# Routing tables made tile by tile, weight loads that wait for a gather, and two copies on another engine

## The chip, the cores and the metric

The kernel runs on one core of a Trainium2 chip. The metric is the device time of one launch in microseconds; it is the median of several runs.

## The reference

Attention, then a routed expert layer, then a dense layer. The shapes are 4 batches x 12 heads x 448 rows x 64; 1792 tokens of 768 numbers; 8 experts with room for 224 tokens each, 768 to 1024 to 768; and a dense 768 to 2048 to 768.

```python
q_n, k_n = rmsnorm(q, g_q), rmsnorm(k, g_k)
attn = softmax(q_n @ k_n.T / 8)
x = tokens(attn @ v)                       # 1792 x 768

cap = N // E                               # 224
logits = x @ w_gate                        # 1792 x 8
for idx in np.argsort(-logits.flatten()):  # best pairs first
    tok, e = idx // E, idx % E
    if assigned[tok] >= 0 or counts[e] >= cap:
        continue
    assigned[tok] = e
    counts[e] += 1
for e in range(E):
    out[assigned == e] = np.maximum(x[assigned == e] @ w1[e], 0) @ w2[e]

h = out @ w_in
return np.where(h > 0, h, np.exp(np.minimum(h, 0)) - 1) @ w_out
```

Every token ends with exactly one expert, and each expert with exactly 224 tokens. The loop over all pairs is sequential; the kernel finds the same assignment in another way.

## The kernel before, in words

The program has four stages: attention (to about 280 us), the routing (280 to 309), the eight experts, and the dense layer. Weights and operands are kept as a high and a low f16 part, and each product is made of three f16 matmuls.

**Routing.** The token's logits lie as L, 128 partitions x 14 token tiles x 8 experts. A round (`round_`, called five times) lets each token choose its best expert (`choose`, oh), and then raises the prices of the experts that are too full (`raises`). For that it counts, for each expert, how many of its tokens would stay at each of 128 price steps. The count is a sum of matmuls, one for each token tile: the weights are a table of 128 x 128 comparisons (token against step), and the moving operand is oh of that tile, with 8 columns. Two tiles' tables, ga, are made by ScalarE (ACT) with a sign function; twelve tiles' tables, gd, by VectorE (DVE). The counts (cnt) give ind on DVE, and two small matmuls k and q end the round. Between these, TensorE runs filler matmuls named warm on operands that nobody reads. Beside them DVE makes halves of the first expert's low weight parts, named wa (`W.low`), and ACT their high parts (`W.high`).

**Placing.** `place` numbers the tokens of each expert (pre), and splits the number into hi and lo. The tables Pm, 128 tokens x 112 places for each of 14 tiles, are comparisons of lo with the numbers 0 to 111; 14 matmuls (ip) with them give, for each expert and place, the token that belongs there. DVE turns these into idx. It also makes fi, which tells whether the assignment is complete. If it isn't, a conditional block with more rounds runs; on these inputs it is passed by.

**Gather and first expert.** `gather()` fetches the 224 rows of an expert by two indirect DMAs on POOL's queue, into xg, half 1 first and then half 0. It is called for the first expert straight behind the placing, for the second behind the conditional. `columns(0)` then makes f16 parts xh on ACT and DVE, transposes them on TensorE (xt) and copies them to xe; the first expert's matmuls are ph (first layer) and py (second).

**Weights of the later experts.** `W.split` issues a load into a staging tile (fw, five of them), and orders ACT's and DVE's conversions behind `W.after`. The instructions of each engine are ordered by a scheduler, except in the blocks marked `manual_schedule`; `issue_after(x)` makes the scheduler place what is issued in it behind x.

**Queues.** A load by SyncE (SP) goes to one of its eight DMA semaphores DMAHW0 to DMAHW7, indirect DMAs on POOL to DMASW0 and following.

Of the kernel before, what the change touches and what calls it, by code (L numbers as in the profile page):

```python
# [6 lines left out]
F16 = mybir.dt.float16  # L7
I32 = mybir.dt.int32
AF = mybir.ActivationFunctionType
ALU = mybir.AluOpType  # L10
# [10 lines left out]
P = 128  # L21
# [9 lines left out]
def attention(tc, qk_d, v_d, qT_d, g_d, idh, idn_d, R_d, xs, L, route, W, npairs=NP_):  # L31
    nc = tc.nc
    order = [(s.split(":")[0], int(s.split(":")[1])) for s in ORDER.split()]
    with tc.tile_pool(name="ac", bufs=1) as cp, \
# [381 lines left out]
        with tc.manual_schedule():  # L416
            first()
            for t in range(lo_, npairs + hi_):
                if t == 1:
                    gate()  # L420
                turn(t)
                if t == npairs - 5:
                    route.rows()
                if npairs - 4 <= t <= npairs:
                    W.load()

# [70 lines left out]
def host_route():  # L497
    G, D, Q = route_grids()
    p = np.arange(P)
    tok = np.zeros((P, NT + 1), np.float32)  # L500
    tok[:, NT] = np.where(p < P - 1, CAP - 0.5, -1)
    for t in range(NT):
        if t < 12:
            tok[:, t] = (t // 3) * S + (t % 3) * P + p
        else:
            tok[:, t] = (2 * (t - 12) + (p >= 64)) * S + 384 + p % 64
    ar = np.ascontiguousarray
    c16 = np.concatenate([np.broadcast_to(G.reshape(1, -1), (P, 3 * P)), np.triu(np.ones((P, P)), 1), np.ones((P, P)),
                          np.repeat(np.stack([D, Q], 1).reshape(6, P).T, P, axis=1)], axis=1).astype(np.float16)
    rows = np.repeat(np.concatenate([G[0], G[1], np.arange(112, dtype=np.float16)]), 8)  # L510
    return dict(c16=ar(c16), c32=ar(tok), c8=ar(np.broadcast_to(rows, (P, len(rows)))))


class Route:
    def __init__(self, tc, cp, ring, c16_d, c32_d, c8_d):
        self.tc, self.nc = tc, tc.nc
        nc = tc.nc
        self.ring, self.c8_d = ring, c8_d
# [12 lines left out]
    def constants(self):  # L531
        for a, b in self.loads:
            self.nc.sync.dma_start(a, b)

    def rows(self):

        GG = self.ring.tile([P, 2, P, 8], F16, tag="w2", name="GG", bufs=6)
        self.io = self.ring.tile([P, 112, 8], F16, tag="w2", name="io", bufs=6)
        self.GG = [GG[:, n] for n in range(2)]
        self.nc.sync.dma_start(GG.rearrange("p n c t -> p (n c t)"), self.c8_d[:, 0:16 * P])  # L540
        self.nc.sync.dma_start(self.io.rearrange("p c t -> p (c t)"), self.c8_d[:, 16 * P:])

    def windows(self, sp, pp, L):

# [24 lines left out]
    def run(self, L, idx, row_d, W, gather):  # L569
# [9 lines left out]
        with tc.tile_pool(name="rt", bufs=1, reuse_waits="tile") as sp, \  # L579
# [6 lines left out]
            oh, half, ga, gd = T("oh", tile3, F16), T("half", [P, A, 8], F16), T("ga", [P, A, P], F16), T("gd", [P, P, NT - A], F16)  # L586
            U, V, M, s, v, u = T("U", tile3), T("V", tile3), T("M", tile3), T("s", tile3), T("v", [P, NT]), T("u", [P, NT], F16)
# [19 lines left out]
            def raises(X, n, *beside):  # L607


                for h in H:  # L610
                    nc.vector.scalar_tensor_tensor(s[:, h], X[:, h], 1000.0, oh[:, h], ALU.min, ALU.mult)

                nc.scalar.activation(half, oh[:, 0:A], AF.Copy, scale=0.5)
                for h in H:
                    nc.vector.tensor_reduce(u[:, h], s[:, h], AX.X, ALU.max)
                for t in range(A):
                    nc.scalar.activation(ga[:, t], self.G[n], AF.Sign, bias=u[:, t:t + 1], scale=-1.0)
                for h in H:
                    a, b = max(h.start, A), h.stop
                    G = self.GG[n][:, :, 0:b - a] if n < 2 else self.G[n].unsqueeze(2).broadcast_to([P, P, b - a])  # L620
                    nc.vector.tensor_tensor(gd[:, :, a - A:b - A], u[:, a:b].unsqueeze(1).broadcast_to([P, P, b - a]), G, ALU.is_ge)
                for f in beside:
                    f()
                cnt = pp.tile([P, 8], F32, name="cnt", tag="cnt")
                for t in range(A):
                    nc.tensor.matmul(cnt, self.ones, half[:, t], start=t == 0, stop=False)
                for t in range(NT):
                    nc.tensor.matmul(cnt, ga[:, t] if t < A else gd[:, :, t - A], half[:, t] if t < A else oh[:, t], start=False, stop=t == NT - 1)
# [16 lines left out]
            def place(first=lambda: None, second=lambda: None):  # L645
# [13 lines left out]
                r1, pos, hi, lo = T("r1", tile3), T("pos", [P, NT]), T("hi", [P, NT]), T("lo", [P, NT], F16)  # L659
                Pm, Q = T("Pm", [P, 112, NT], F16), T("Qm", [P, NT, 2, 8], F16)  # L660
# [7 lines left out]
                nc.vector.scalar_tensor_tensor(lo, hi, -112.0, pos, ALU.mult, ALU.add)  # L668
                nc.gpsimd.tensor_tensor(Q[:, :, 1], Q[:, :, 0], hi.unsqueeze(2).broadcast_to(tile3), ALU.mult)
                ip = pp.tile([112, 2, 8], F32, name="ip", tag="ip")  # L670
                for h in H:
                    n = h.stop - h.start
                    nc.vector.tensor_tensor(Pm[:, :, h], lo[:, h].unsqueeze(1).broadcast_to([P, 112, n]), self.io[:, :, 0:n], ALU.is_equal)
                nc.vector.tensor_scalar(j, pre[0:1, NT, :], CAP, None, ALU.is_equal)
                nc.vector.tensor_reduce(f, j, AX.X, ALU.add)
                nc.vector.tensor_copy(fi, f)
                second()

                for t in range(NT):
                    nc.tensor.matmul(ip, Pm[:, :, t], Q[:, t], start=t == 0, stop=t == NT - 1)  # L680
# [14 lines left out]
            with tc.manual_schedule():  # L695
                for h in H:
                    nc.vector.tensor_tensor(U[:, h], L[:, h], bc(self.t0, h.stop - h.start), ALU.subtract)
                warm(8)
                round_(0, L, self.iw, W.high, relative)
                for k in range(1, KSTEP):  # L700
                    round_(1, Ln, self.r, W.high, W.low)
                choose(Ln)
                fi = place(lambda: W.low(2), lambda: W.low(4))
                gather()
                W.second(2)
                for k in range(3):
                    W.high()
                    W.low(2)
                warm(3)
# [59 lines left out]
class Weights:  # L769
# [51 lines left out]

    def split(self, tag, bufs, src, n, name):
        nc = self.nc
        f = self.stage(src, n, name)
        w = self.ring.tile([P, 2, n], F16, tag=tag, name=name, bufs=bufs)
        with self.tc.issue_after(self.after):
            nc.scalar.activation(w[:, 0], f, AF.Copy, scale=SW)  # L827
        with self.tc.issue_after(self.after):
            nc.vector.scalar_tensor_tensor(w[:, 1], f, SW, w[:, 0], ALU.mult, ALU.subtract)  # L829
        return w  # L830
# [44 lines left out]
class Rows:  # L875
# [5 lines left out]
    def gather(self, e=0, x=None):  # L881
        x = x or self.first
        for h in (1, 0):
            self.nc.gpsimd.indirect_dma_start(x[h][0:112], None, self.xs, bass.IndirectOffsetOnAxis(ap=self.idx[0:112, h, e:e + 1], axis=0))
        return x


def moe(tc, xp, pre, xs, idx, idh, W, rows, ring, w1_d, w2_d, wi_d, wo_d, lin, g_d, t_d, out):
    nc = tc.nc
    with tc.tile_pool(name="mp", bufs=1, space=PSUM, reuse_waits="tile") as pp:  # L890
# [19 lines left out]
        with tc.tile_pool(name="m1", bufs=1, reuse_waits="tile") as sp:  # L910
# [5 lines left out]
            def columns(e):  # L916
# [9 lines left out]
                for d in range(0, 6, 2):  # L926
                    pt = bank(2 if e == 0 and d == 4 else 0, f"xt{e}_{d}").bitcast(F16)[:, 0:4 * CAP].rearrange("p (d j c) -> p d j c", d=2, j=2)
                    for k in range(2):
                        for h in (1, 0):
                            for j in range(2):  # L930
                                nc.tensor.transpose(pt[:, k, j, 112 * h:112 * h + 112], hl[h][0:112, j, (d + k) * P:(d + k + 1) * P], idh[0:112, 0:112])  # L931
                    last = nc.vector.tensor_copy(x[:, d:d + 2], pt)  # L932
                return last.ins

            def result(e, d, ps):
# [255 lines left out]
```

## Time and profile before

| | |
|---|---|
| runs | 968.62, 969.22, 968.42 us; median 968.62 |
| profiled execution | 968.6 us, span 966.8 us |
| TensorE (PE) busy | 938.5 us, 97% of the span |
| VectorE (DVE) busy | 727.0 us, 75% |
| ScalarE (ACT) busy | 521.8 us, 54% |
| GpSimd (POOL) busy | 295.3 us, 31% |

All times of the trace count from the start of the span. The slices of the page divide the span into 40 equal parts, and a digit 9 means busy for nine tenths or more. In a timeline, each row is one instruction or several like ones in succession (x4), with its start, the time that it covers, and in brackets how long the engine was idle before it and what ended that.

### The profile page before, as it was taken

The page shows a single profiled execution, that of the slowest core. Times are in us where ns is not written, and L with a number is a line of the kernel's source. Part 1 is how long each engine was busy: PE and PEld are TensorE (multiplying, and loading weights), DVE is VectorE, ACT ScalarE, POOL GpSimd, SP SyncE. Part 2 cuts the span into 40 slices and gives each one's busy share as a digit, 9 for nine tenths or more (in the row PEclk, how much of TensorE's full clock was granted, in tenths as well). Part 3 has the DMA queues.
Part 4 walks back from the last instruction along what each step waited for, and adds up shares of the span by engine and source line. Part 5 has one row for each costly group of instructions (what it writes and reads, how often), then busy time and mean ns, then how long its engine had stood idle before and what let it go on. Part 6 is the DMA issues. An engine that isn't in the chain of part 4 may idle for free.

```text
span 966.8 us, 18734 instructions
## 1 busy us (share of the span) xinstructions
PE 938.5 (97%) x6920; PEld 624.0 (65%) x6920; DVE 727.0 (75%) x1424; ACT 521.8 (54%) x1148; POOL 295.3 (31%) x483
## 2 busy tenths in 40 slices
PE   5999999999998999999999999999999999999997
PEld 2465555555554889999999955555555566666664
DVE  6899999899867898787878799999834675555430
ACT  4899998999853666666655243343312323333320
POOL 6889999999521532221000000000000000000000
PEclk8999999999998999999999999999999999999999
DMA  9444434453235788777765377787764563333000
GB/s 333 182 126 124 154 118 139 131 172 91 59 112 162 180 286 280 243 228 244 223 211 178 104 253 254 256 259 263 208 215 124 161 224 112 105 114 99 33 33 33
DMA packets 100640, 164.93 MB, mean 171 GB/s; under 512 B 32960, under 2 KB 66240, under 8 KB 100160
## 3 DMA queue, kind: packets, MB, share of 16 engines
q1 hardware_dynamic: 96336, 152.66, 50.1%
q0 software_dynamic: 2400, 11.01, 3.3%
q8 instruction: 56, 0.92, 0.4%
q10 hardware_dynamic: 1808, 0.01, 0.1%
q14 instruction: 40, 0.33, 0.1%
HBM read 131.66 MB, written 31.99 MB: 169 GB/s over the span
## 4 chain that ended last, share of the span: by engine, by line
PE 88%; DVE 5%; ACT 2%; DMA 2%; issue 1%; POOL 1%; POOLq 0%; DVEq 0%; ACTq 0%
PE l L1076 23%; PE o_b L1123 11%; PE py L997 10%; PE ph L960 10%; PE o L305 8%; PE o_c L1123 6%; PE s L228 6%; PE pt L281 5%; PE o_a L1123 3%; PE s L221 1%; PE pt L279 1%; PE pk L198 1%; DVE w L829 1%; PE xt L931 1%; PE xo L329 1%
## 5 line engine op out<-in xcount | busy, mean ns | idle before, releaser
L1076 PE MATMUL l<-xc,wic 128*128 128x384 f16 (+1 forms) x1152 | 218.2, 353 | 0.0
L1076 PEld LDWEIGHTS <-wic 128*128 128x128 f16 x1152 | 112.7, 98 | 104.8
L1139 POOL DMA_INDIRECT out<-xc,id x14 | 13.7, 982 | 463.7 <-issue 311.7
L1123 PEld LDWEIGHTS <-a 128*128 128x128 f16 x1080 | 105.7, 98 | 69.8
L829 DVE SCALAR_TENSOR_TENSOR w<-fw,w 128x768 f16<-128x768 f32 (+1 forms) x98 | 112.8, 1153 | 25.2 <-ACT w L827 25.1
L997 PE MATMUL py<-h,w 128*128 128x224 f16 x1152 | 113.8, 259 | 1.5 <-DVE h L962 1.5
L233 DVE TENSOR_REDUCE s<-s 128x1 f32<-128x448 f32 x168 | 105.2, 626 | 9.6 <-PE s L228 8.9
L997 PEld LDWEIGHTS <-w 128*128 128x128 f16 x1152 | 109.9, 98 | 1.9 <-issue 1.6
L252 ACT ACTIVATE p<-s,nb,r 128x448 f32<-128x448 f32 x144 | 104.4, 726 | 4.8 <-DVE nb L239 3.5
L960 PE MATMUL ph<-xe,w 128*128 128x224 f16 x1008 | 99.1, 259 | 0.7 <-DVE xe L932 0.4
L960 PEld LDWEIGHTS <-w 128*128 128x128 f16 x1008 | 96.5, 98 | 1.1 <-issue 1.1
L827 ACT ACTIVATE w<-fw 128x768 f16<-128x768 f32 (+1 forms) x98 | 90.7, 928 | 3.2 <-DMA fw<-w 3.0
L290 ACT ACTIVATE e<-pt 128x448 f32<-128x448 f32 (+2 forms) x216 | 83.7, 428 | 15.8 <-PE pt L281 15.2
L1078 ACT ACTIVATE e<-l 128x512 f32<-128x512 f32 (+1 forms) x64 | 34.5, 539 | 100.5 <-PE l L1076 100.5
L305 PE MATMUL o<-e,v 128*64 128x448 f32 x384 | 87.8, 558 | 0.0
L281 PE MATMUL pt<-idn,p 128*128 128x128 f32 x432 | 70.9, 276 | 2.1 <-ACT p L252 1.6
L281 PEld LDWEIGHTS pt<-idn,p 128*128 128x128 f32 x432 | 50.1, 140 | 24.5 <-ACT e L290 16.7
L924 POOL TENSOR_TENSOR xh<-xg,xh 112x768 f16<-112x768 f32 x14 | 25.7, 1853 | 122.3 <-ACT xh L923 122.3
L1053 DVE SCALAR_TENSOR_TENSOR a<-s,a 128x1024 f16<-128x1024 f32 (+2 forms) x30 | 33.4, 1116 | 38.6 <-ACT a L1052 38.6
L228 PE MATMUL s<-ks,qh 128*128 128x448 f16 x144 | 51.8, 360 | 7.6 <-ACT p L252 6.5
L1123 PE MATMUL o_b<-wb,a 128*128 128x384 f16 x312 | 51.8, 326 | 0.0
L228 PE MATMUL s<-ks,ql 128*128 128x448 f16 x144 | 51.4, 357 | 0.0
(244 smaller groups left out, 1605.0 us busy)
## 6 DMA issues: line engine op xcount, KB each, us to landing
fw<-w SPq DMA_DIRECT2D x56, 384.0 KB, 3.8
fw<-w SPq DMA_DIRECT2D x42, 512.0 KB, 4.6
xwi<-wi SPq DMA_DIRECT2D x16, 768.0 KB, 4.7
xwo<-wo SPq DMA_DIRECT2D x16, 768.0 KB, 4.7
q<-g_d SPq DMA_DIRECT2D x24, 512.0 KB, 3.7
qT<-qT SPq DMA_DIRECT2D x24, 448.0 KB, 4.2
qk<-qk SPq DMA_DIRECT2D x23, 448.0 KB, 3.5
g_d<-e SPq DMA_DIRECT2D x32, 256.0 KB, 4.8
```

Source lines behind the costliest of these rows:

```text
L228: nc.tensor.matmul(ps[:, 0:448], q[:, o:o + P], ks[:, 448 * h:448 * h + 448], start=n == 0, stop=n == 1)
L233: nc.vector.tensor_reduce(d["s", u][:, 448:449], d["s", u][:, 0:448], AX.X, ALU.max, negate=True)
L252: nc.scalar.activation(dst, d["s", u][:, 0:448], AF.Exp, bias=d["nb", u], scale=d["r"][:, rc:rc + 1], accum_out=d["sm"][:, rc:rc + 1])
L281: nc.tensor.transpose(pt[:, j * P:(j + 1) * P], p[j][:, h, 64 * h + c * P:64 * h + (c + 1) * P], idn)
L290: move = nc.vector.tensor_copy if u not in (0, 1, 2, 4, 5, 6) else lambda o, x: nc.scalar.activation(o, x, AF.Copy)
L305: nc.tensor.matmul(d["o"][64 * h:64 * h + 64, 0:448], d["v"][:, c + 4 * h, :], d["e", min(2 * c + h, 6)], start=c == 0, stop=c == 3)
L827: nc.scalar.activation(w[:, 0], f, AF.Copy, scale=SW)
L829: nc.vector.scalar_tensor_tensor(w[:, 1], f, SW, w[:, 0], ALU.mult, ALU.subtract)
L960: mm = nc.tensor.matmul(ps, w[:, i, d * P:(d + 1) * P], x[:, d, j], start=d == 0 and n == 0, stop=d == 5 and n == 2)
L997: nc.tensor.matmul(ps, w[:, i, f * P:(f + 1) * P], h[:, f, j], start=f == 0 and n == 0, stop=f == 7 and n == 2)
L1076: nc.tensor.matmul(ps, w[:, i, d * P:(d + 1) * P], xc[cb][:, h, d, j], start=d == 0 and m == 0, stop=d == 5 and m == 2)
L1123: nc.tensor.matmul(ps, a[x][:, f, i], wt[b][f][:, j], start=first and f == 0 and k == 0, stop=f == 7 and k == 2, skip_group_check=True)
```

## The change

- **Tables of a round.** gd and Pm are laid out by token tile, so that one tile's table is contiguous. Each tile's table is made by one DVE operation that compares a whole row of steps with one number per partition: u for gd (12 operations instead of 2 in a round), lo for Pm (14 instead of 2). u and lo become f32. The 14 count matmuls stand in another order.
- **Constants.** The repeated tables GG and io, loaded in attention's last part, are gone. A small io of 112 numbers is loaded instead.
- **Loads of the second expert.** gather() of the first expert is followed by a DMA of one number from the gathered half 0 to a scratch row. It is named `W.behind`, and all loads in `W.split` are ordered behind it.
- **Copies.** For the first expert, two of three copies of xe (d = 0 and 4) go to ACT.

```diff
-                for h in H:
-                    a, b = max(h.start, A), h.stop
-                    G = self.GG[n][:, :, 0:b - a] if n < 2 else ...
-                    nc.vector.tensor_tensor(gd[:, :, a - A:b - A], u[:, a:b].unsqueeze(1).broadcast_to([P, P, b - a]), G, ALU.is_ge)
+                for t in range(A, NT):
+                    nc.vector.tensor_scalar(gd[:, t - A], self.G[n], u[:, t:t + 1], None, ALU.is_le)
...
-                for t in range(NT):
-                    nc.tensor.matmul(cnt, ga[:, t] if t < A else gd[:, :, t - A], ...)
+                for t in (2, 3, 4, 5, 0, 6, 7, 8, 9, 1, 10, 11, 12, 13):
+                    nc.tensor.matmul(cnt, ga[:, t] if t < A else gd[:, t - A], ...)
...
-                for h in H:
-                    n = h.stop - h.start
-                    nc.vector.tensor_tensor(Pm[:, :, h], lo[:, h].unsqueeze(1).broadcast_to([P, 112, n]), self.io[:, :, 0:n], ALU.is_equal)
+                for t in range(NT):
+                    nc.vector.tensor_scalar(Pm[:, t], io, lo[:, t:t + 1], None, ALU.is_equal)
...
-                gather()
+                W.behind = nc.sync.dma_start(row_d[0:1, 0:1], gather()[0][0:1, 0:1]).ins
...
     def split(self, tag, bufs, src, n, name):
         nc = self.nc
-        f = self.stage(src, n, name)
+        with self.tc.issue_after(self.behind):
+            f = self.stage(src, n, name)
...
-                    last = nc.vector.tensor_copy(x[:, d:d + 2], pt)
+                    last = nc.scalar.activation(x[:, d:d + 2], pt, AF.Copy) if e == 0 and d != 2 else nc.vector.tensor_copy(x[:, d:d + 2], pt)
```

The instructions as they stand in the built programs show three places. The first is DVE in one of the later rounds, from the maxima u to ind. Before:

```order
L615 TENSOR_REDUCE u<-s 128x6
L615 TENSOR_REDUCE u<-s 128x8
L621 TENSOR_TENSOR gd<-u,GG 128x128x4
L621 TENSOR_TENSOR gd<-u,GG 128x128x8
L794 SCALAR_TENSOR_TENSOR wa_4913<-fa_4160,wa_4913 128x384
L629 TENSOR_SCALAR ind<-cnt,c_72 128x8
```

And DVE in the same round of the changed kernel:

```order
L606 TENSOR_REDUCE u<-s 128x6
L606 TENSOR_REDUCE u<-s 128x8
L610 TENSOR_SCALAR gd<-c_71,u 128x128 x12
L782 SCALAR_TENSOR_TENSOR wa_4921<-fa_4156,wa_4921 128x384
L618 TENSOR_SCALAR ind<-cnt,c_72 128x8
```

Twelve operations stand where two stood; the half of wa behind them, and ind behind that, have not moved.

The second place is SP at the conditional, with what each instruction waits for (fi is the flag of the placing; fw_1_0 and fw_1_1 are the first two weight loads of the second expert). Before:

```order
L694 TENSOR_LOAD fi [waits DVE_49]
L694 ISA x2
L819 DMA fw_1_0_6975<-w 128x768 [waits DMAHW2_49,DVE_49,Activation_49]
L819 DMA fw_1_1_7001<-w 128x768 [waits DMAHW3_49,DVE_49,Activation_49]
L711 COMPARE_AND_BRANCH
...
L711 UNCONDITIONAL_BRANCH [waits SP_sequencer_49,DMAHW0_49,DMAHW1_49,DMAHW2_49,DMAHW3_49,DMAHW4_49,DMAHW5_49,DMAHW6_49,DMAHW7_49]
```

And SP in the changed kernel:

```order
L682 TENSOR_LOAD fi [waits DVE_49]
L682 ISA x2
L692 DMA row<-xg_0_4826 1x1 [waits DMAHW1_49,DMASW1_49]
L807 DMA fw_1_0_7100<-w 128x768 [waits DMAHW2_49,DVE_49,Activation_49]
L807 DMA fw_1_1_7126<-w 128x768 [waits DMAHW3_49,DVE_49,Activation_49]
L699 COMPARE_AND_BRANCH
```

The copy to row stands ahead of both loads and waits for DMASW1, the semaphore of the gather's second DMA. The loads still stand ahead of the conditional, behind which SP waits for all eight of its semaphores.

The third place is ACT behind the conditional, with its waits: the f16 parts xh of the gathered halves. Before:

```order
L923 ACTIVATE xh_1_6541<-xg_1_4831 112x256 [waits DMASW2_49,DMAHW5_49,DMASW0_49,DVE_49]
L923 ACTIVATE xh_1_6541<-xg_1_4831 112x256 x2
L923 ACTIVATE xh_0_6540<-xg_0_4830 112x256 [waits DMASW3_49,DMASW1_49,DVE_49]
L923 ACTIVATE xh_0_6540<-xg_0_4830 112x256 x2
L953 DMA lin<-ix_6509 112x16x1 [waits DMAHW1_49,DVE_49]
```

And ACT in the changed kernel:

```order
L912 ACTIVATE xh_1_6666<-xg_1_4827 112x256 [waits DMASW2_49,DMAHW5_49,DMASW0_49,DVE_49]
L912 ACTIVATE xh_1_6666<-xg_1_4827 112x256 x2
L912 ACTIVATE xh_0_6665<-xg_0_4826 112x256 [waits DMASW3_49,DMASW1_49,DVE_49]
L912 ACTIVATE xh_0_6665<-xg_0_4826 112x256 x2
L921 ACTIVATE xe_6664<-xt_0_6679 128x896 [waits DMAHW5_49,PE_49]
L921 ACTIVATE xe_6664<-xt_4_6699 128x896 [waits PE_49]
L942 DMA lin<-ix_6634 112x16x1 [waits DMAHW1_49,DVE_49]
```

The first xh waits for the same semaphores as before, DMAHW5 among them; the two copies of xe come behind xh.

## Rows read from the trace of the kernel before

**Rows 1.** The page's 40 slices: TensorE's busy tenths.

```profile
PE   5999999999998999999999999999999999999997
```

**Rows 2.** Windows: us; PE, PEld, DVE, ACT, POOL busy (instructions); PEclk, DMA share, GB/s.

```profile
331.00:350.00 19.00, 16.31 (x178) 15.67 (x176) 19.00 (x20) 13.11 (x22) 13.19 (x8) 1.00 0.86 257
```

**Rows 3.** Timeline of the last round: start, us, engine and line, tiles, count.

```profile
299.18 1.02 DVE L621 TENSOR_TENSOR gd<-u,GG 128x512 f16<-128x512 f16 x2
...
299.96 0.96 PE L628 MATMUL cnt<-oh,gd 128*128 128x8 f16 x12
300.12 0.55 DVE L794 SCALAR_TENSOR_TENSOR wa<-fa,wa 128x384 f16<-128x384 f32 x1
...
300.96 0.23 DVE L629 TENSOR_SCALAR ind<-cnt,c 128x8 f16<-128x8 f32 x1 [0.29 <-PE cnt L628]
```

**Rows 4.** Timeline of the placing.

```profile
304.72 1.18 DVE L673 TENSOR_TENSOR Pm<-lo,io 128x672 f16<-128x672 f16 x2
...
305.42 2.99 PE L680 MATMUL ip<-Qm,Pm 128*112 128x16 f16 x14 [0.60 <-DVE Pm L673]
...
306.26 1.94 DVE L794 SCALAR_TENSOR_TENSOR wa<-fa,wa 128x384 f16<-128x384 f32 x4
308.45 0.17 DVE L682 TENSOR_SCALAR idx<-ip 112x8 int32<-112x8 f32 x1 [0.25 <-PE ip L680]
```

**Rows 5.** The chain that ended last, 306 to 322 us: start, us, step.

```profile
308.92 6.21 DMA xg<-xs,idx
...
315.20 0.42 ACT xh L923
```

**Rows 6.** DVE groups by form, whole span: count, busy us, mean ns; idle before.

```profile
L1079 DVE TENSOR_SCALAR e<-e 128x512 f32<-128x512 f32 x32 | 13.3, 416 | 12.8 <-ACT e L1078 12.8
L1079 DVE TENSOR_SCALAR e<-e 128x384 f32<-128x384 f32 x32 | 11.2, 350 | 14.9 <-ACT e L1078 14.9
L1044 DVE TENSOR_TENSOR s<-s,q 128x1024 f32<-128x1024 f32 x6 | 7.3, 1223 | 0.2
L621 DVE TENSOR_TENSOR gd<-u,GG 128x1024 f16<-128x1024 f16 x5 | 3.4, 684 | 0.0
```

**Rows 7.** Timeline of DVE, 36.4 to 37.4 us, in attention.

```profile
36.51 0.68 DVE L207 TENSOR_SCALAR qh<-qT,G 128x896 f16<-128x896 f32 x1
37.10 0.15 DVE L239 TENSOR_TENSOR nb<-s,r 128x1 f32<-128x1 f32 x1
```

**Rows 8.** DMAs from issue to landing: gathers L884, scatters L1139, weight loads L819.

```profile
DMA to landing us min/median/max: 5.6/7.0/8.8
DMA to landing us min/median/max: 3.0/3.0/4.8
DMA to landing us min/median/max: 3.0/4.1/6.8
```

**Rows 9.** Timeline of POOL: the second gather DMA of the first expert.

```profile
310.38 0.93 POOL L884 DMA_INDIRECT xg<-xs,idx  x1 [0.30 <-POOLq L711]
```

**Rows 10.** SP's signals at L711, three stretches: count, ns, from and to.

```profile
L711 SPq EVENT_SEMAPHORE  x3: 17/17/17, 310.0 to 310.2; - x3
...
L711 SPq EVENT_SEMAPHORE  x1: 17/17/17, 311.3 to 311.3; - x1
...
L711 SPq EVENT_SEMAPHORE  x5: 17/17/17, 314.0 to 314.3; - x5
```

**Rows 11.** Windows (columns as in the second group) around the gather.

```profile
307.00:313.80 6.80, 5.40 (x17) 2.54 (x18) 3.65 (x10) 0.70 (x1) 2.09 (x2) 0.50 0.72 200
313.80:317.20 3.40, 2.80 (x16) 1.13 (x13) 2.58 (x7) 1.95 (x6) 2.02 (x2) 1.00 0.69 193
```

**Rows 12.** Timeline of TensorE: the fillers ahead of the first expert.

```profile
311.11 4.94 PE L949 MATMUL warm<-wa,idh 128*128 128x512 f16 x16 [1.40 <-PEq L711]
```

**Rows 13.** Groups by form: a conversion on ACT, the copies of xe on DVE.

```profile
L827 ACT ACTIVATE w<-fw 128x768 f16<-128x768 f32 x56 | 46.6, 837 | 3.2 <-DMA fw<-w 3.0
...
L932 DVE COPY xe<-xt 128x896 f16<-128x896 f16 x24 | 14.7, 617 | 3.3 <-PE xt L931 3.2
```

More of the change, by code (lines that the diff above doesn't have):

```diff
@@ L421, in attention @@
                 turn(t)
-                if t == npairs - 5:
-                    route.rows()
                 if npairs - 4 <= t <= npairs:
@@ L509, in host_route @@
                           np.repeat(np.stack([D, Q], 1).reshape(6, P).T, P, axis=1)], axis=1).astype(np.float16)
-    rows = np.repeat(np.concatenate([G[0], G[1], np.arange(112, dtype=np.float16)]), 8)
-    return dict(c16=ar(c16), c32=ar(tok), c8=ar(np.broadcast_to(rows, (P, len(rows)))))
+    return dict(c16=ar(c16), c32=ar(tok), c8=ar(np.broadcast_to(np.arange(112, dtype=np.float16), (P, 112))))
 class Route:
@@ L517, in __init__ @@
         nc = tc.nc
-        self.ring, self.c8_d = ring, c8_d
+        self.c8_d = c8_d
         c16 = cp.tile([P, 11 * P], F16, name="c16")
@@ L533, in constants @@
             self.nc.sync.dma_start(a, b)
[L535 to L541, printed above, removed]
     def windows(self, sp, pp, L):
@@ L585, in run @@
             A = 2
-            oh, half, ga, gd = T("oh", tile3, F16), T("half", [P, A, 8], F16), T("ga", [P, A, P], F16), T("gd", [P, P, NT - A], F16)
-            U, V, M, s, v, u = T("U", tile3), T("V", tile3), T("M", tile3), T("s", tile3), T("v", [P, NT]), T("u", [P, NT], F16)
+            oh, half, ga, gd = T("oh", tile3, F16), T("half", [P, A, 8], F16), T("ga", [P, A, P], F16), T("gd", [P, NT - A, P], F16)
+            U, V, M, s, v, u = T("U", tile3), T("V", tile3), T("M", tile3), T("s", tile3), T("v", [P, NT]), T("u", [P, NT])
+            io = T("io", [P, 112], F16)
+            nc.sync.dma_start(io, self.c8_d)
             self.r = T("r", [P, 8])
@@ L617, in raises @@
                     nc.scalar.activation(ga[:, t], self.G[n], AF.Sign, bias=u[:, t:t + 1], scale=-1.0)
-                for h in H:
-                    a, b = max(h.start, A), h.stop
-                    G = self.GG[n][:, :, 0:b - a] if n < 2 else self.G[n].unsqueeze(2).broadcast_to([P, P, b - a])
-                    nc.vector.tensor_tensor(gd[:, :, a - A:b - A], u[:, a:b].unsqueeze(1).broadcast_to([P, P, b - a]), G, ALU.is_ge)
+                for t in range(A, NT):
+                    nc.vector.tensor_scalar(gd[:, t - A], self.G[n], u[:, t:t + 1], None, ALU.is_le)
                 for f in beside:
@@ L626, in raises @@
                     nc.tensor.matmul(cnt, self.ones, half[:, t], start=t == 0, stop=False)
-                for t in range(NT):
-                    nc.tensor.matmul(cnt, ga[:, t] if t < A else gd[:, :, t - A], half[:, t] if t < A else oh[:, t], start=False, stop=t == NT - 1)
+                for t in (2, 3, 4, 5, 0, 6, 7, 8, 9, 1, 10, 11, 12, 13):
+                    nc.tensor.matmul(cnt, ga[:, t] if t < A else gd[:, t - A], half[:, t] if t < A else oh[:, t], start=False, stop=t == NT - 1)
                 nc.vector.tensor_scalar(ind, cnt, self.full, None, ALU.is_ge)
@@ L658, in place @@
                 j, f, fi = T("j", [1, 8]), T("f", [1, 1]), T("fi", [1, 1], I32)
-                r1, pos, hi, lo = T("r1", tile3), T("pos", [P, NT]), T("hi", [P, NT]), T("lo", [P, NT], F16)
-                Pm, Q = T("Pm", [P, 112, NT], F16), T("Qm", [P, NT, 2, 8], F16)
+                r1, pos, hi, lo = T("r1", tile3), T("pos", [P, NT]), T("hi", [P, NT]), T("lo", [P, NT])
+                Pm, Q = T("Pm", [P, NT, 112], F16), T("Qm", [P, NT, 2, 8], F16)
                 first()
@@ L679, in place @@
                 for t in range(NT):
-                    nc.tensor.matmul(ip, Pm[:, :, t], Q[:, t], start=t == 0, stop=t == NT - 1)
+                    nc.tensor.matmul(ip, Pm[:, t], Q[:, t], start=t == 0, stop=t == NT - 1)
                 nc.vector.tensor_scalar(idx[0:112, 1], ip[:, 1], N - 1, None, ALU.min)
```

## The prediction

> **What bounds the kernel now.** I read the page first, then the busy times by stage, then the routing stage operation by operation. TensorE is busy nine tenths or more in nearly every slice [rows 1]. There nothing that this change touches can help or hurt. It is not the bound in the routing stage, from 280 to 320 us: its matmuls there are mostly the fillers named warm, and the chain that ended last runs through DVE, ACT and the gather. So each microsecond by which the first expert's matmuls (ph) start later moves the end. Nothing takes it back: behind, DVE is busy 19.00 of 19 us (331 to 350) with the next expert's weights [rows 2], and that work is itself released by the first expert's results.
>
> A round lasts 3.92 us. In the last one DVE makes the tables gd in 0.94 us (299.18 to 300.12), then a weight half wa (0.55), then waits 0.29 for the counts [rows 3]. What ends last there is TensorE, with the twelve gd matmuls at 0.08 each (0.96 in all). In the placing step DVE makes both Pm in 1.10 us (304.72 to 305.82), TensorE needs 2.99 us for the 14 matmuls ip on them, and DVE, which has four more halves of wa ahead of idx, waits only 0.25 for TensorE [rows 4]. The gather then takes 6.21 us from its start at 308.92, and ACT starts xh at 315.20 [rows 5].
>
> **What one gd or Pm operation costs.** The trace has no f16 TENSOR_SCALAR of 128 elements, so I build its price. Without a per-partition operand, 512 and 384 elements of f32 take 416 and 350 ns [rows 6]: 0.52 ns an element and 150 ns fixed. L207 has such an operand, as the new ones do, and takes 0.68 us for 896 elements [rows 7], which leaves 210 fixed: the operand adds 60 ns. A two-input operation of 1024 elements takes 1223 ns in f32 and 684 in f16 [rows 6], little over half. I carry that over and halve the time of an element: 128 x 0.26 = 33 ns. L207's successor starts 0.59 us after it, 0.09 before its recorded end [rows 7]. One operation then holds DVE for 210 + 33 less 80 to 90, and I take 160 ns. Bounds: 193 ns if f16 gains nothing (128 x 0.52 = 67), 100 ns if the operand's 60 ns lie beside the operation before. I take the middle, since each of its parts rests on a row.
>
> The Trainium skill (VectorE: DVE Perf Modes, section "The TRN2 errata") gives 58 cycles plus the elements over a factor of up to four: an estimate of 94 ns for this operation, with which the routing would gain 0.7 us instead of losing the 3.7 below. The same section warns that the fixed part is paid per tile and advises tiles of 512 elements or more, which speaks against this change. Its figure for L207 would be 527 ns; the trace has 0.59 us, so here the row decides.
>
> **Rounds.** Twelve operations take 12 x 0.16 = 1.92 us in place of 0.94. In a round that starts gd at g, the half wa follows at g + 1.92 and holds DVE 0.47 (0.55 less 0.08), so ind can start at g + 2.39; now it starts at g + 1.78 (300.96). TensorE is no longer last: the last gd is done at g + 11 x 0.16 + 0.24 = g + 2.00, and load, matmul and signal add about 0.3. That is +0.61 in each of four rounds. In the first round only the short vn stands behind gd and TensorE ends it, at g + 2.3: about +0.55. Sum +3.0. The cheaper weight loads from contiguous tables and the new matmul order are hidden behind DVE.
>
> **Placing.** 14 x 0.155 = 2.17 us for Pm in place of 1.10: +1.07 on DVE. The contiguous Pm shorten TensorE's 2.99 us, but the four halves of wa still stand ahead of idx, and of the slack only the wait of 0.25 and 0.08 of overlap are given back: +0.75. Routing together: +3.7 us. By the bounds: +6.1 at 193 ns (rounds 5 x (12 x 0.033 + 0.6) = 5.0, placing 0.75 + 14 x 0.033 = 1.2, less 0.1 for the first round), -0.7 at 100 ns (12 x 0.06 = 0.72 less in each round, five times 0.12 under now, placing -0.1).
>
> **The gather and the join.** Without the weight loads the gather lands earlier. Now its second half needs 5.6 us at the least from issue, while the late scatters of the same rows, L1139, need 3.0 [rows 8]. With s the start of the first gather (308.92), the second is issued at s + 1.46 [rows 9] and lands between s + 4.5 and s + 7.1; I take s + 5.3, nearer to the undisturbed row. Only then does SP issue the small copy to row, then fw_1_0 and fw_1_1, at about 0.5 us each: fw_1_1 goes out at s + 6.4.
>
> This is where the change runs into a wait. The two loads stand ahead of the conditional, and behind it SP passes its DMA queues one by one, each when all that was sent on it has landed. SP's signals at L711 show it: three at 310.0 to 310.2, one at 311.3, and five from 314.0 to 314.3 [rows 10]; fw_1_0 and fw_1_1 are on the fourth and fifth. By the order rows ACT's first xh and DVE's xh wait for queue DMAHW5, which SP passes after DMAHW2 and DMAHW3. Now that wait ends by 314.3 and is hidden by the gather, which lands at 315.13 [rows 5]. Afterwards it cannot be: fw_1_1 is only issued when the whole gather has landed. Weight loads land 3.0, 4.1, 6.8 us after issue (least, median, most) [rows 8]; the gathers for the second expert now run beside them, so at the median fw_1_1 lands at s + 10.5 and xh starts at s + 10.7, against s + 6.28 now: **+4.4 us** (bounds s + 8.8 and s + 15.2: +2.5 and +8.9). Queued behind are POOL's third gather, which waits for SP, the rest of SP's loads, and with xh all of the first expert.
>
> **Clock.** TensorE's granted clock is at its lower level (1.2 of 2.4 GHz) from 307.0 to 313.8, where TensorE is busy 5.40 of 6.80 us, and at 2.4 GHz after it [rows 11], 2.7 us after the warm matmuls began at 311.11. These 16 last 4.94 us [rows 12]. With xh 4.4 us later TensorE stands idle for some 4 us before ph, so I expect the lower level again, for 2.7 us of dense work, which loses 1.35 us (bounds 0 and 3.4, half of the 6.8 us stretch).
>
> **The rest.** Copies of xe: ACT needs 837 ns for 768 elements, some 0.94 us for 896, DVE 0.62 [rows 13]. The first copy ends 0.3 us later; the second runs on DVE beside it, 0.25 earlier, so the twelve matmuls that need the first two end together as before: 0. If they did not overlap: 0.3. The 0.7 MB that GG and io no longer load lay under attention, where TensorE is at nine tenths or more [rows 1]: 0, and 3.7 us without that cover, at the 200 GB/s of [rows 11]. Moving the last half of wa ahead of the branch costs DVE 0.94 us while xh waits anyway: 0.
>
> **Sum.** The profiled execution took 968.6 us, the median of three is 968.62, so no correction is needed: 968.6 + 3.7 + 4.4 + 1.35 = **978.1 us**.
>
> **Rivals.**
> 1. The operand's time is hidden, 100 ns an operation (the page's estimate is near it). For it: neighbouring operations do overlap by 0.09 [rows 7], and the operand could be fetched in that time; against it: L207 has its operand, overlaps, and still holds DVE for 0.59. Routing -0.7: 968.6 - 0.7 + 4.4 + 1.35 = 973.7 us.
> 2. The routing gets dearer still: f16 gains nothing where only one input is an array, and 193 ns give 968.6 + 6.1 + 5.75 = 980.5. For it: the f16 gain is carried over from another form of operation; against it: nothing in these rows.
> 3. The other side: the join holds nothing, xh starts as the first gather lands. It decides whether ACT's first xh starts before fw_1_1 has landed. At s + 4.0 (between L1139's 3.0 and 6.21 now) xh gains 2.3 us and the clock is as now: 968.6 + 3.7 - 2.3 = 970.0 us, no measurable change; with the cheap operations too, 968.6 - 0.7 - 2.3 = 965.6, faster. For it: today the join hides behind the gather. Against it: SP's signals stop exactly where the loads are.
>
> **Chances and numbers.** A measurement of this kernel tells about 0.2% (1.9 us) from no change. Forecast 0.54 (975.5 to 982), rival 1 0.21, rival 2 0.12, rival 3 0.13, of which 0.06 with the cheap operations. The likeliest gives 978.1. The range from 971.5 to 983.0 leaves out rival 3 and the ends of the bounds, under 2 in 10. Faster is the second form of rival 3: 0.06; no change its first: 0.07; slower the other three: 0.87.
>
> **What would show it.** Right: 60 gd operations at starts 0.16 apart; rounds of 4.5 us; idx later by 3.7; a wait of ACT's xh over 9 us with the weight loads landing just before it; a TensorE gap of about 4 us behind warm, then a lower clock. Wrong: gd starts 0.10 apart and rounds of 3.8 us (rival 1), ACT's xh starting within 1 us of the gather's landing (rival 3), gd 0.19 apart (rival 2).

## The result, and the profile after

The changed kernel takes 983.07 us (median of five runs, 981.26 to 985.57) against 968.62 us: a ratio of 1.0149, with a 95% interval from 1.0132 to 1.0166. It is slower by 14.5 us, on the side that was forecast, but the size lies beyond the range: 978.1 us had been predicted, with 983.0 as its end. The profiled execution has a span of 981.3 us against 966.8, so it shows the whole 14.5.

The page's slices of TensorE and of its granted clock show where to look: in the 13th and 14th (294 to 343 us) TensorE is busy 7 tenths, at 6 and 7 tenths of its clock.

```profile
PE   5999999999997789999999999999999999999997
PEclk7999999999996799999999999999999999999999
```

The timeline of the last round and of the placing, the counterparts of [rows 3, 4]:

```profile
301.82 2.03 DVE L610 TENSOR_SCALAR gd<-c,u 128x128 f16<-128x128 f16 x12
303.77 0.55 DVE L782 SCALAR_TENSOR_TENSOR wa<-fa,wa 128x384 f16<-128x384 f32 x1
304.24 0.22 DVE L618 TENSOR_SCALAR ind<-cnt,c 128x8 f16<-128x8 f32 x1
...
307.98 2.39 DVE L661 TENSOR_SCALAR Pm<-io,lo 128x112 f16<-128x112 f16 x14
...
308.36 2.32 PE L668 MATMUL ip<-Qm,Pm 128*112 128x16 f16 x14 [0.28 <-DVE Pm L661]
...
312.60 0.15 DVE L670 TENSOR_SCALAR idx<-ip 112x8 int32<-112x8 f32 x1
```

Twelve gd operations hold DVE for 303.77 - 301.82 = 1.95 us, 162 ns each, in place of 0.94. Neither ind nor idx has a bracket any more: DVE no longer waits for TensorE, it ends each step itself. The 14 cheaper ip matmuls (2.32 us, before 2.99) don't help either, since DVE still has its halves of wa ahead of idx.

The gather, the loads and the join (the point behind the conditional where SP passes all its queues), the counterparts of [rows 5, 9, 10]: timelines of POOL, SP and ACT, then SP's signals.

```profile
313.04 1.16 POOL L873 DMA_INDIRECT xg<-xs,idx  x1 [4.78 <-DVE idx L671]
314.50 0.93 POOL L873 DMA_INDIRECT xg<-xs,idx  x1 [0.30 <-POOLq L699]
318.90 0.94 POOL L873 DMA_INDIRECT xg<-xs,idx  x1 [3.46 <-DVEq L699]
320.14 0.94 POOL L873 DMA_INDIRECT xg<-xs,idx  x1 [0.30 <-issue]
321.56 0.94 POOL L873 DMA_INDIRECT xg<-xs,idx  x1 [0.48 <-issue]
322.80 0.93 POOL L873 DMA_INDIRECT xg<-xs,idx  x1 [0.30 <-issue]
```

```profile
319.28 0.30 SPq L692 DMA_DIRECT2D row<-xg  x1
319.69 6.53 SPq L807 DMA_DIRECT2D fw<-w  x3
```

```profile
325.74 1.64 ACT L912 ACTIVATE xh<-xg 112x256 f16<-112x256 f32 x5 [14.76 <-SPq L699]
```

```profile
L699 SPq EVENT_SEMAPHORE  x3: 17/17/17, 320.8 to 320.9; - x3
...
L699 SPq EVENT_SEMAPHORE  x1: 17/17/17, 324.2 to 324.2; - x1
...
L699 SPq EVENT_SEMAPHORE  x5: 17/17/17, 325.5 to 325.8; - x5
```

The first two rows of POOL are the first expert's gather, the other four those of the second and third expert. The copy to row goes out 6.24 us after the first gather's start (s), when the second half has landed. The two loads follow, beside the later gathers; SP signals fw_1_0 at 324.2 and fw_1_1 at 325.5, and ACT's xh, whose wait now ends with SP and not with the gather, starts at 325.74 = s + 12.70. Before it was s + 6.28.

The third difference is TensorE's granted clock. In the windows of the second fence (columns as in [rows 2]) it is at its lower level from 309.9 to 320.1, and again from 324 to 333.5. The first fence has what TensorE did before that second stretch: the fillers, and then 4.75 us in which it waited for xh. The clock fell in that time.

```profile
315.56 5.90 PE L938 MATMUL warm<-wa,idh 128*128 128x512 f16 x16 [3.58 <-PEq L699]
326.21 0.27 PE L920 MATMUL xt<-idh,xh 112*128 112x112 f16 x1 [4.75 <-ACT xh L912]
```

```profile
283.00:302.00 19.00, 17.19 (x109) 8.79 (x108) 17.73 (x110) 7.49 (x22) 2.07 (x5) 0.85 0.55 194
...
309.90:320.10 10.20, 6.62 (x19) 2.52 (x20) 5.99 (x19) 0.84 (x1) 3.03 (x3) 0.50 0.28 75
324.00:333.50 9.50, 6.64 (x45) 5.42 (x46) 2.81 (x8) 4.07 (x9) 0.00 (x0) 0.50 0.93 249
```

And ACT waits longer for one weight load of the next expert, here and, in the second fence, in the kernel before:

```profile
370.61 0.84 ACT L816 ACTIVATE w<-fw 128x768 f16<-128x768 f32 x1 [3.00 <-DMA fw<-w]
```

```profile
356.32 0.84 ACT L827 ACTIVATE w<-fw 128x768 f16<-128x768 f32 x1 [1.59 <-DMA fw<-w]
```

The 14.5 us of the profile, stage by stage, from the starts of such rows: from the first round to s 27.06 became 31.25 us (+4.2); s to xh +6.4; xh to DVE's first h (the first expert's first result) 6.05 became 7.87 us (+1.8); the first two experts behind it +2.1, of which 0.5 are the end of the low clock and the rest begins at that load; behind the second expert nothing differs.

### The profile page after: what moved, and what is told of

It is laid out like the page before. It is cut to its first block, busy times and chain, and to the rows that moved or that the text cites. A ratio compares the mean times of both kernels' runs of the same rounds, so it can differ in the third digit from the quotient of the medians.

```text
span 981.3 us, 18797 instructions
## 1 busy us (share of the span) xinstructions
PE 945.4 (96%) x6920; PEld 625.7 (64%) x6920; DVE 731.9 (75%) x1484; ACT 524.3 (53%) x1150; POOL 295.1 (30%) x483
## 4 chain that ended last, share of the span: by engine, by line
PE 62%; DVE 2%; issue 1%; DMA 1%; ACT 0%; POOLq 0%; DVEq 0%; ACTq 0%
PE l L1065 22%; PE o_b L1112 11%; PE ph L949 10%; PE py L986 10%; PE o_c L1112 6%; PE o_a L1112 3%; DVE w L818 1%; PE xt L920 1%; DMA fw<-w 1%; DMA out<-xc,id 0%; ACT xh L912 0%; DVE h L951 0%; DVE w L803 0%; DVE xe L921 0%; ACT w L816 0%
```

## The experiments

Theory: the DVE operations cost some 4 us, the join 6.4, the clock behind it 2.3, and one late load the rest. Rival A: the longer rounds, in which the granted clock falls (0.85 above), cost most of it. All medians with their own runs of the kernel before on the same chip:

| kernel | us | before | ratio (95%) | first round to s | s to xh | xh to first h |
|---|---|---|---|---|---|---|
| before | 968.62 | | | 27.06 | 6.28 | 6.05 |
| changed | 983.07 | 968.62 | 1.0149 (1.0132 to 1.0166) | 31.25 | 12.70 | 7.87 |
| e1 no wait | 975.82 | 969.76 | 1.0065 (1.0052 to 1.0078) | 31.28 | 7.64 | 6.01 |
| e2 wait alone | 977.06 | 969.76 | 1.0074 (1.0061 to 1.0087) | 27.10 | 12.52 | 6.78 |
| e3 copies alone | 969.49 | 969.76 | 0.9999 (0.999 to 1.0008) | 27.07 | 5.54 | 7.89 |
| e4 behind join | 974.94 | 969.76 | 1.0052 (1.0039 to 1.0065) | 32.75 | 4.64 | 7.92 |
| e5 gd alone | 974.19 | 969.86 | 1.0037 (1.0023 to 1.0051) | 31.92 | 5.93 | 6.48 |
| e6 Pm alone | 972.13 | 969.86 | 1.0022 (1.0013 to 1.0031) | 27.94 | 5.43 | 7.97 |
| e7 38 fillers | 982.44 | 969.86 | 1.0120 (1.0104 to 1.0135) | 31.27 | 13.78 | 7.18 |
| e8 before, behind join | 970.27 | 969.86 | 1.0000 (0.999 to 1.0011) | 27.07 | 4.48 | 7.78 |
| e10 order alone | 969.29 | 969.65 | 0.9993 (0.9984 to 1.0002) | 27.29 | 5.70 | 6.10 |
| e11 changed again | 985.47 | 969.65 | 1.0159 (1.0144 to 1.0174) | 31.28 | 13.39 | 6.69 |
| e12 44 fillers | 983.52 | 969.65 | 1.0138 (1.0123 to 1.0154) | 32.73 | 15.05 | 6.93 |
| e13 gathers later | 980.99 | 969.31 | 1.0117 (1.0101 to 1.0132) | 32.87 | 11.55 | 7.12 |
| e14 9 fillers | 970.19 | 969.31 | 1.0010 (1.0001 to 1.0019) | 27.01 | 5.89 | 7.32 |

The last three columns are of the one profiled execution of each. That is the slowest of its kernel's executions for e4, e8, e12 and e13, and the runs of before that stand beside the experiments have medians 0.7 to 1.2 us above the first one. So a difference of about 1 us between two profiles tells nothing by itself.

**e1: the changed kernel without the wait.**

```diff
-                W.behind = nc.sync.dma_start(row_d[0:1, 0:1], gather()[0][0:1, 0:1]).ins
+                gather()
...
-        with self.tc.issue_after(self.behind):
-            f = self.stage(src, n, name)
+        f = self.stage(src, n, name)
```

> The changed kernel, only without the copy to row and without the order of the loads behind it. Theory (routing costs 4.2 us, and the loads that land late hold the whole conditional's end, 6.4 us, with 2.3 us of clock and 1.5 us of later loads in its wake): only the routing is left, 968.6 + 4.2 = 972.8 us (971.5 to 974.5), and ACT's first xh starts about 6.3 us after the first gather does. Rival A (the longer rounds, in which the granted clock falls, cost most of the 14.5 us): 978 us or more.

Measured +6.1 us: eight of the 14.5 us go with the wait, so rival A falls as the main cause. But it is 2 us more than expected. In the profile 1.4 of it is the join again, without any order: fw_1_1 landed late, 7.7 us after its issue, and SP's signal that ended ACT's wait came at s + 7.6.

**e2: the wait alone, in the kernel before.** The edit is the change's own two places (`W.behind = ...` behind the placing, `issue_after(self.behind)` in `split`).

> The kernel before with the copy to row and the order of the loads behind it alone. Theory: 968.6 + 6.4 + 2.3 + 1.5 = 978.8 us (976.5 to 980.5), xh about 12.7 us after the first gather's start. Rival A: 972 us or less. If the clock's loss needs the routing too: 976.5.

Measured +7.3 us, 3 less than the 10.2 expected. The join is there in full (s to xh 12.52), of the clock 0.7 in place of 1.8, and the late load isn't there. Of POOL's later gathers only one runs beside the two loads here; the next waits for SP:

```profile
322.13 1.01 POOL L885 DMA_INDIRECT xg<-xs,idx  x1 [6.26 <-SPq L711]
```

e1 and e2 together give 13.4 of 14.5.

**e3: the copies on ACT alone** (the change's one line).

> The kernel before with the two copies of xe on ACT alone. Theory: within 0.5 us of 968.6, since the second copy runs beside the first. Rival: the slower ACT copy is waited for, 969.0 to 969.5.

No difference that can be told: the interval reaches from 1 us faster to 0.8 slower, so the term of 0 fits, and 0.3 couldn't be told from it. In its profile TensorE does wait 1.01 us for the second copy on ACT:

```profile
321.48 11.09 PE L960 MATMUL ph<-xe,wa 128*128 128x224 f16 x114 [1.01 <-ACT xe L932]
```

The profile of the changed kernel has no such gap; there ph runs in one piece.

**e4: the same wait, but issued behind the conditional.**

```diff
-                W.behind = nc.sync.dma_start(row_d[0:1, 0:1], gather()[0][0:1, 0:1]).ins
+                W.row, W.got = row_d, gather()
...
                 gather(1)
+                W.behind = nc.sync.dma_start(W.row[0:1, 0:1], W.got[0][0:1, 0:1]).ins
```

> The changed kernel, with the copy to row issued behind the conditional and not ahead of it, so that the loads still wait for the gather but nobody waits for the loads at the conditional. Theory (the wait hurts by its place ahead of the conditional): about as without the wait, 972.8 us (971.5 to 975), xh about 6.3 us after the first gather's start. Rival B (it hurts because the second expert's weights come late, wherever the wait stands): 977 us or more, though xh is early.

975 us, as e1: the loads still wait for the gather, and hardly anything is lost by it, so rival B falls here. What cost 7 to 9 us (e1, e2 and this run) was that the conditional's end waits for them. xh starts at s + 4.64, not 6.3 as expected: the first half of the gather, with no weight loads beside it, lands 1.6 us sooner than in the kernel before. The gain isn't seen at the end: xh to h takes 7.92 us, because the 16 fillers, at the lower clock, are still running.

```profile
317.88 5.93 PE L939 MATMUL warm<-wa,idh 128*128 128x512 f16 x16 [3.95 <-PEq L699]
323.65 1.35 PE L920 MATMUL xt<-idh,xh 112*128 112x112 f16 x24
```

All 24 transposes run in one piece behind the last filler.

**e5 and e6: the tables gd alone (with the matmul order), and Pm alone, in the kernel before.** Of the edits the new loops are shown; the old ones go, and the layouts and types change with them as in the change.

```diff
+                for t in range(A, NT):
+                    nc.vector.tensor_scalar(gd[:, t - A], self.G[n], u[:, t:t + 1], None, ALU.is_le)
```

```diff
+                for t in range(NT):
+                    nc.vector.tensor_scalar(Pm[:, t], io, lo[:, t:t + 1], None, ALU.is_equal)
```

> The kernel before with the tables gd tile by tile and the new matmul order alone. Theory (162 ns an operation on DVE's path, 0.66 us in each round): 3.3 us slower than before, and the gather as now: 971.9 us beside 968.6 (3.0 to 4.0 us slower). Rival A (the clock that falls in the longer rounds holds up the warm matmuls and with them the counts): 4.5 us slower or more, with ind waiting for TensorE in some rounds.

> The kernel before with the tables Pm tile by tile alone. Theory: 14 x 0.162 in place of 1.10 us, less the wait of 0.25 and an overlap: 0.9 us slower (0.6 to 1.2). If the weight loads, which are issued by the same amount later, then land behind the gather and hold xh: up to 2.2 us slower.

gd alone costs 4.3 us by the medians, 3.6 by the ratio (2.2 to 4.9). In its profile the rounds take 3.3 us more, as worked out, and 1.5 more come in the placing, where TensorE is at the lower clock: the six fillers ahead of pre take 2.60 us (1.46 in the profiles of the changed kernel and of before), and DVE waits 1.50 for pre.

```profile
305.60 2.60 PE L596 MATMUL warm<-c 128*128 128x512 f16 x6
...
309.52 0.33 DVE L662 TENSOR_TENSOR r<-oh,pre 128x48 f32<-128x48 f16 x2 [1.50 <-PE pre L654]
```

So rival A is right in a part of it: not the counts wait for TensorE, but pre does. The windows of the rounds, from 283 to 302 us, show it for e5 and for e10, which keeps the old tables:

```profile
283.00:302.00 19.00, 17.25 (x113) 8.79 (x113) 17.73 (x111) 7.28 (x20) 2.41 (x6) 0.91 0.57 200
302.00:309.00 7.00, 6.58 (x41) 3.20 (x39) 5.77 (x31) 4.79 (x9) 0.64 (x2) 0.77 0.17 57
```

```profile
283.00:302.00 19.00, 15.81 (x135) 9.57 (x133) 15.87 (x75) 8.93 (x25) 2.08 (x6) 1.00 0.56 196
```

Of the kernels here, all nine with gd tile by tile have 0.85 to 0.91 in this window, and all seven with the old tables 1.00. The order of the matmuls isn't the reason (e10); whether it is the longer rounds or the new layout of the tables, no run tells apart. In the rounds themselves the low clock costs nothing (19.6 us became 22.9 in each of the nine, wherever the clock was low), since DVE ends them. Where a low stretch reaches into the placing it costs 1.5 to 1.6 us, which it did in five of the nine profiles.

Pm alone costs 2.3 us by the medians (2.1 by the ratio, 1.3 to 3.0), not 0.9: the placing takes 0.9 us more, as worked out. Where the rest comes from stays open. In its profile xh to h takes 1.9 more, while the 16 fillers take 6.42 us in place of 4.94 and end at 320.07, long behind xh (316.39). But xh starts 0.9 sooner (s + 5.4, so the join took no part), and e3, which is as fast as before, has nearly the same two numbers (5.54 and 7.89).

**e7 and e12: more fillers in the changed kernel,** 38 and 44 for 16; e11 is the changed kernel once more.

```diff
-                for _ in range(16):
+                for _ in range(38):
                     nc.tensor.matmul(warm, ...)
```

> The changed kernel with 38 filler matmuls ahead of the first expert instead of 16, so that TensorE doesn't stand idle before xh. Theory (2.3 us of the loss are the lower clock behind the idle 4.75 us): 981 us beside 983 (1.3 to 2.6 us faster than the changed kernel), the transposes xt in 1.2 instead of 2.14 us. Rival C (behind xh the engines wait for each other, not for the clock): within 0.5 us of the changed kernel.

> The changed kernel once more, on the same chip as the next one. Theory: 13 to 15 us slower than before, with the rounds 22.9 us long and xh 12.7 us behind the first gather's start, as in its first profile; the weight load that was 1.4 us late in expert 1 may land in time here.

> The changed kernel with 44 filler matmuls ahead of the first expert, 6 more than in the run with 38, so that they reach to xh. Theory (the lower clock behind the idle time costs 2.3 us): 1.5 to 2.6 us faster than the changed kernel of the same call, and no stretch at the lower clock behind xh. Rival C: within 0.5 us of it.

Inconclusive by the times: both lie 1 to 4 us below the two runs of the changed kernel (1.0120 and 1.0138 against 1.0149 and 1.0159), but of their intervals only that of e7 is clear of one of the two, e11's. The transposes took 1.21 us in e7, as expected, and 2.02 in e12. The clock's stretch behind xh became shorter, but did not go: in the windows of e7 it is up from 321 to 330, and down again for 3.2 us with ph running; in e12 it is down from 332.8 to 336.1.

```profile
321.00:330.00 9.00, 7.05 (x48) 3.47 (x47) 2.15 (x7) 2.39 (x7) 2.18 (x3) 1.00 0.95 275
330.80:334.00 3.20, 3.20 (x19) 2.53 (x18) 0.00 (x0) 0.52 (x2) 0.00 (x0) 0.50 0.77 172
```

What the clock cost behind xh is 0.6 to 1.8 us in the six profiles with the join (xh to h; e9, with its added work, left out), with more fillers or without. e11 is 15.8 us slower than before, 0.8 more than expected. It repeats the stages up to xh, with a later join (13.39), and has another late weight load in the first two experts.

**e8: e4's edit in the kernel before.**

> The kernel before, with the second expert's loads behind a copy to row that is issued behind the conditional. Theory (nobody waits at the conditional for loads, and the first gather, alone on the DMA engines, lands 4.6 instead of 6.2 us after its start): 0.5 to 1.5 us faster than before. Rival B (the second expert's weights come 8 us later and are waited for): no gain, or up to 2 us slower.

No change (0.999 to 1.0011), where 0.5 to 1.5 us of gain were expected. xh starts at s + 4.48, 1.8 us earlier, and the fillers take 1.7 of it (xh to h 7.78). Later the second expert's weights are waited for, 6.59 us on ACT:

```profile
343.20 0.84 ACT L828 ACTIVATE w<-fw 128x768 f16<-128x768 f32 x1 [6.59 <-DMA fw<-w]
```

So rival B's wait is there, and no gain is what it forecast. How much the wait costs as a rule isn't shown: this profile is of the slowest of the twelve executions (972.82 us).

**e9: prices on DVE,** one execution (992.17 us, since the added work delays xh).

```diff
+                for t in range(8):
+                    nc.vector.tensor_scalar(ds[:, 0:P], g0[:, 0:P], 100.0, None, ALU.is_le)
+                for t in range(8):
+                    nc.vector.tensor_scalar(ds[:, 0:P], g0[:, 0:P], tk[:, t:t + 1], None, ALU.is_le)
+                for t in range(6):
+                    nc.vector.tensor_scalar(ds, g0[:, 0:512], tk[:, t:t + 1], None, ALU.is_le)
+                for t in range(4):
+                    nc.vector.tensor_scalar(df, W.rt.ones32, tk[:, t:t + 1], None, ALU.is_le)
```

> The changed kernel with 26 more DVE operations, whose results nobody reads, where DVE waits for xh: 8 TENSOR_SCALAR of 128 f16 elements with a constant, 8 with an operand for each partition, 6 of 512 f16 elements with such an operand, 4 of 128 f32 elements with it. By the prediction's price (operand 60 ns, 0.26 ns an f16 element, 0.52 an f32 one) their starts are 0.10, 0.16, 0.26 and 0.195 us apart. Rival: the operand costs nothing and the operation's fixed part is the larger, 0.16 with a constant too.

The added operations of one kind write the same tile, and each waited for the one before, so that their starts say nothing (0.23 and 0.29 us for the first two kinds); their durations do (groups by form):

```profile
L946 DVE TENSOR_SCALAR dum<-c,c 128x512 f16<-128x512 f16 x6 | 2.1, 353 | 0.2
L944 DVE TENSOR_SCALAR dum<-c,c 128x128 f16<-128x128 f16 x8 | 2.0, 254 | 0.3
L942 DVE TENSOR_SCALAR dum<-c 128x128 f16<-128x128 f16 x8 | 1.6, 195 | 10.7 <-SPq L699 10.4
L948 DVE TENSOR_SCALAR duf<-ones,c 128x128 f32<-128x128 f32 x4 | 1.1, 286 | 0.1
```

The operand costs 254 - 195 = 59 ns, an f16 element (353 - 254) / 384 = 0.26 ns, and 128 f32 elements 32 ns more than f16 ones: the three numbers of the prediction. The fixed part, 254 - 59 - 33 = 162 ns, is 12 more than the 150 it worked out, and the overlap in the changed kernel, 254 - 162 = 92 ns, a little more than its 80 to 90, so that the 160 came out right.

**e10: the matmul order alone, in the kernel before.**

```diff
-                for t in range(NT):
+                for t in (2, 3, 4, 5, 0, 6, 7, 8, 9, 1, 10, 11, 12, 13):
```

> The kernel before with the new order of the count matmuls alone. Theory (in the kernel before TensorE ends the round, since the twelve gd matmuls stand behind the second ga): ind no longer waits 0.29 us for the counts, 0.15 to 0.3 us a round, 0.7 to 1.4 us faster. Rival: the last eight tables are made at once, so that their matmuls can't start earlier: no change (within 0.3 us).

No change that can be told (0.9993, 0.9984 to 1.0002). By the time alone 0.7 us faster would fit too; the profile speaks against it: from the first round to s it takes 27.29 us, no less than before. The last eight gd matmuls wait for the second DVE operation, and ind still waits for the counts:

```profile
300.70 0.41 PE L628 MATMUL cnt<-oh,gd 128*128 128x8 f16 x4 [0.17 <-DVE gd L621]
```

**e13: the changed kernel, with the next experts' gathers behind the first expert's xe.**

```diff
-                gather(1)
...
                 nc.vector.tensor_copy(ix2[0:112], idx[0:112])
+                rows.idx = ix2
+                gather(1)
```

> The changed kernel, with the gathers for the second and third expert issued behind the first expert's xe, so that they don't run beside the two weight loads that the conditional's end waits for. Theory (the join was 2 to 4 us dearer than forecast because these gathers slow the loads): fw_1_1 lands 3.5 to 4.2 us after its issue instead of 5.5 to 7.3, xh starts 11 to 11.5 us after the first gather's start instead of 12.7 to 15, 1.5 to 3 us faster than the changed kernel. Rival D (the loads are slow by themselves, so soon after the gather): xh as late as in the changed kernel.

980.99 us; the ratio is 1.0117 (to 1.0132) against 1.0149 (from 1.0132) and 1.0159 (from 1.0144), so 3 to 4 us of the loss are gone. In the profiles 1.2 to 1.8 of them are at the join (s to xh 11.55 against 12.70 and 13.39). In the first fence SP issues the two loads (0.83 us for both, the second some 0.47 behind the first), in the second it signals them:

```profile
322.08 0.83 SPq L807 DMA_DIRECT2D fw<-w  x2
```

```profile
L699 SPq EVENT_SEMAPHORE  x1: 17/17/17, 325.2 to 325.2; - x1
L699 SPq EVENT_SEMAPHORE  x5: 17/17/17, 326.1 to 326.4; - x5
```

fw_1_1 lands 326.1 - 322.55 = 3.6 us after its issue, although the gather itself took 6.8 us here. The time from its issue to its landing in the changed kernel, in e2 and here:

```profile
DMA to landing us min/median/max: 5.3/5.3/5.3
DMA to landing us min/median/max: 5.0/5.0/5.0
DMA to landing us min/median/max: 3.6/3.6/3.6
```

With one later gather beside it (e2) the load took about as long as with several. Rival D falls: the loads were slow because the gathers for the second and third expert ran beside them.

**e14: nine fillers in the kernel before.**

```diff
-                for _ in range(16):
+                for _ in range(9):
```

> The kernel before with 9 filler matmuls ahead of the first expert instead of 16. Theory (where the fillers run at the lower clock they end behind xh and hold the transposes, up to 1.8 us): equal or up to 1 us faster. Rival: without the fillers the clock is not back when ph starts, 1 to 2 us slower.

Slightly slower (1.0010, from 1.0001). The fillers end at 314.28, the clock falls at 317, and xt takes 2.14 us at the lower level:

```profile
310.82 3.46 PE L949 MATMUL warm<-wa,idh 128*128 128x512 f16 x9 [1.03 <-PEq L711]
```

```profile
314.00:317.00 3.00, 0.72 (x4) 0.19 (x2) 2.14 (x6) 1.49 (x5) 2.13 (x2) 1.00 0.80 255
317.00:320.20 3.20, 3.01 (x27) 2.70 (x28) 2.89 (x7) 0.56 (x2) 2.19 (x3) 0.50 1.02 264
```

With 16 at the lower clock it is the fillers that end late. None of these versions beats the kernel before.

## Why the prediction was right in kind and wrong in size

- **Price of an operation: right.** 160 ns forecast, 162 measured, and its parts (60 and 33 ns) by e9. Rivals 1 (100 ns) and 2 (193 ns) fall. The estimate of 94 ns from the Trainium skill (VectorE: DVE Perf Modes, section "The TRN2 errata") does not hold here. The same section adds, which the prediction left out, that its formula comes out too low for a single operation. Its warning against many small tiles holds: twelve of them took 1.95 us in place of 0.94.
- **Rounds and placing: nearly right.** +3.0 and +0.75 forecast, +3.3 and +0.9 measured. Left out was that the rounds with the new tables let the clock fall, which I had looked for only in the trace of before; where the low stretch meets the placing it costs up to 1.6 us more (e5, e13), though not in the changed kernel's own two profiles.
- **The join: right mechanism, mis-sized term, the step that failed.** The prediction put the second half's landing at s + 5.3 and "at the median fw_1_1 lands at s + 10.5": +4.4 us. Measured in five profiles of kernels with this join and the gathers as they are (e9 left out): xh at s + 12.5 to s + 15.1, +6.2 to +8.8, and +6.4 in the changed kernel's first profile. The second half landed at s + 6.2 with hardly anything beside it, 4.8 us after its issue: the scatters' 3.0 were no measure for it. And fw_1_1 took 5.0 us (e2) to 7.0 (e12), 5.3 in that profile, not the median of 4.1: the text named the gathers that run beside the loads and then took the median of all weight loads. e13 shows 3.6 us without them. Of the 2.0 us that were missing in that profile, 0.9 are the landing and 1.2 the load; 0.2 came back, since fw_1_1 went out 0.9 us behind the landing, not 1.1. The sentence that POOL's third gather waits for SP did not come true either: it went out at 318.90, ahead of both loads.
- **Clock: right in kind.** 1.35 forecast, 2.3 in the profile (1.8 to the first h, 0.5 behind it), 0.6 to 1.1 to the first h in the other five. The copies on ACT are not the reason: e1 has them and takes 6.01 us from xh to h.
- **A term that was missing.** The late weight load in the second expert (ACT's wait of 3.00 in place of 1.59) adds some 1.5 us. It differs from execution to execution: e2 has none of it, e11 more. And 1.59 is a low value: at the loads of the same place the profiles of e3, e10 and e14, which are as fast as before or nearly so, wait 1.84 to 2.63 us, those with both the tables and the wait 2.20 to 3.00. So much of this term may be the difference of two executions and no work of the change; one profile of each kernel doesn't tell.
- **The rest: right as far as can be told.** Copies (e3) and matmul order (e10) are worth nothing that the times show.
- **Rival 3** (the join holds nothing) fell with the changed kernel's own trace.

The sum of the terms was 9.5 us; in the profile the join brings 2 more, the clock 1, the late load 1.5, the rounds and the placing 0.5. That is the 14.5.

## What to carry to other kernels

Before moving a transfer, look at what stands behind it in program order: a conditional whose end passes all queues turns a load that nobody needs yet into one that everybody waits for, and the same wait behind that point costs nothing that the times show (e4, e8). Price a load by those that run beside the same company, not by the median of all. One operation for each tile pays its fixed part each time: 162 ns for one table, where one two-input operation makes eight of them in 684 [rows 6].

## What the runs showed of the hardware that was not expected

The granted clock of the stretch of rounds from 283 to 302 us was 1.00 in the seven kernels with the old tables and 0.85 to 0.91 in the nine whose rounds were 0.66 us longer, with as many matmuls in each round. Fillers are no safe remedy: with 16 at the lower clock they end behind the data that they should bridge to (e4, e6, e8), with nine the clock fell 2.7 us after their end (e14), and with 38 it fell 4 us after their end, while ph was running (e7). Half a gather, 112 rows, with no weight load beside it landed 4.5 to 5.4 us after its issue (the changed kernel, e4, e7, e8, e12, e13), and 5.2 to 6.2 with two weight loads under way ([rows 5], e3, e6, e10).
